# One load request per tensor for the first batch of an RWKV-5 plus mixer kernel

## The chip, the cores and the metric

The kernel runs on one core of a Trainium2 chip. The metric is device time in microseconds (us) of one execution; three runs of the kernel before the change are given. A core has five engines that each work through their own instructions in order: PE (TensorE, matmuls), DVE (VectorE), ACT (ScalarE), POOL (GpSimd) and SP (SyncE, here only a queue of DMA requests). An engine stops at an instruction whose inputs have not come, and everything behind it on that engine stops with it.

## The reference

Inputs `r`, `k`, `v` have the shape (4 batches, 8 heads, 768 steps, 48), `w` and `u` the shape (8, 48), all float32. Batch by batch a linear attention with decay is computed, and its output goes through a token and channel mixer:

```python
for t in range(S):
    kt, vt, rt = (k[:, :, t], v[:, :, t], r[:, :, t])
    cur = np.einsum('bhd,bhe->bhde', u[None] * kt, vt)
    y[:, :, t] = np.einsum('bhd,bhde->bhe', rt, state + cur)
    state = w[None, :, :, None] * state + np.einsum('bhd,bhe->bhde', kt, vt)
...
h = np.maximum(xt @ w_tok1, 0.0) @ w_tok2
u = x + h.transpose(0, 2, 1)
h2 = np.maximum(u @ w_ch1, 0.0) @ w_ch2
return (u + h2).astype(np.float32)
```

`x` is `y` with the heads side by side, (4, 768, 384); `xt` is its transpose; the mixer's hidden sizes are 256 and 1536.

## The kernel before, in words

The 768 steps of a batch are cut into 6 chunks of 128 steps. For each chunk the kernel multiplies k and r with powers of the decay (into tiles `kr`, bf16), transposes both, makes scores k times r on PE (`at_ps`), masks them on DVE (`AT`), adds the product with v to the product of r with the running state (`y_ps`, `S`, `kv_ps`), and adds the step's own term: `pr` is a product of the transposed k and r, `ad_ps` sums it with u, `adg` is that sum copied, and `yd` or `ydb` is v scaled by it. v is cast to bf16 first (`vb`). The result of a chunk is `x_b`. After the six chunks of a batch comes its mixer: `h_ps<-x_b,wtok` and `hx_ps` (token mixing, weights `wtok1`, `wtok2`), then `z_ps` (up, weights `wch1` in two parts) with a relu into `zr`, then `h_ps<-wch,zr` (down, weights `wch2` in three parts). A `zr` tile has 128 partitions of 12 x 384 bf16, and there are three buffers of it.

Every piece of work is a task made by `add` (line 215) or `flex` (line 222, which takes the engine from the table `ENGINES`). The table `ORDER` (line 21) is the order in which all tasks are emitted, so it sets each engine's order, SP's queue among them. `BUFS` (line 66) names for each pool the buffer that each use takes; a load into a buffer waits until the earlier user of that buffer is done. `kt` and `vt` have six buffers each, `win` three.

For the first two batches (style 'f32') r is read in windows of 256 steps (tile `win`, function `window`, line 558; steps 2p and 2p+1 lie side by side in partition p, so a row in memory is 384 bytes), and k and v by chunks (tiles `kt`, `vt`, line 493; rows of 192 bytes). That makes 15 requests for the first batch: 3 of 384 KB and 12 of 192 KB. SP issues them in this order: r of window 1, r of window 0, k of chunks 1 and 0, r of window 2, k 4, v 3, k 3, k 2, v 1, v 0, k 5, v 2, v 4, v 5. The loads of the second batch follow at their own places in `ORDER`.

The products are `mul_r` (line 561) and `mul_k` (line 794), the cast is `copy_v` (line 798); `turn_k`, `evac_k` and `product` (lines 806, 811, 815) transpose k (`trk`), copy it out of PSUM (`rka`) and make `pr`.

The mixer's seven weight loads (`load_weights`, line 532) are issued by POOL in its own order, each behind a wait for the landing of the load that `W_DEP` (line 173) names as (batch, chunk, 0 for k, 1 for r, 2 for v): both `wtok` parts wait for k of chunk 2, both `wch1` parts for v of chunk 0, and the three `wch2` parts for v of chunk 1, k of chunk 0 and v of chunk 5 of the second batch.

In the profile nearly every instruction has line 278, the helper that all engines are called through, so groups are told apart by tile names.

Of the kernel before, what the change touches and what calls it, by code (L numbers as in the profile page):

```python
# [11 lines left out]
f32 = mybir.dt.float32  # L12
# [6 lines left out]
Ln = ACTF.Ln  # L19

ORDER = [
# [43 lines left out]
]  # L65
BUFS = {
    'AT0': [
# [23 lines left out]
],  # L91
    'krw': [],
    'kt': [
    0, 1, 2, 3, 4, 5, 0, 1, 2, 3, 4, 5, 0, 2, 1, 3, 4, 5, 0, 2, 1, 3, 4, 5,
],
    'ku': [
    0, 1, 2, 0, 1, 2, 0, 2, 1, 0, 1, 0,
# [46 lines left out]
],  # L144
    'vb2': [],
    'vt': [
    0, 1, 2, 3, 4, 5, 0, 1, 2, 3, 4, 5, 0, 1, 2, 3, 4, 5, 0, 1, 2, 3, 4, 5,
],
    'win': [
    0, 1, 2, 0, 1, 2,  # L150
],
    'yd': [
    0, 1, 2, 0, 1, 2, 0, 1, 2, 1, 0, 2, 0, 2, 1, 0, 1, 0,
# [2 lines left out]
    0, 1, 0, 0, 1, 0,  # L156
],
    'zr': [
    0, 1, 2, 1, 0, 2, 1, 2,
],  # L160
}
ENGINES = [
# [9 lines left out]
]  # L172
W_DEP = [(0, 2, 0), (0, 2, 0), (0, 0, 2), (0, 0, 2), (1, 1, 2), (1, 0, 0), (1, 5, 2)]
GATES = {(2, 1, 0): 0, (3, 2, 1): 6}
NWARM = 13
WIDE_AT = [
# [63 lines left out]
def kernel(  # L240
# [14 lines left out]
    B, H, S, D = r.shape  # L255
    dm = H * D
    T = 128
    C = S // T
# [42 lines left out]
    def mul(on, out, a, c):  # L301
        engine_of[on].tensor_mul(out, a, c)
# [8 lines left out]
    def h3(t):  # L311
        return t.rearrange("p (h d) -> p h d", h=H)
# [177 lines left out]
    def two_steps(b, c, i):  # L490
        return (b, c // 2) in PAIRED or (i == 1 and wide(b))

    def load(b, c, i):
        nm, src = (("kt", k), ("rt", r), ("vt", v))[i]
        win = two_steps(b, c, i)
        nm = "win" if win else nm

        def f():
            if win:
                t = sb("win", [128, H, 2 * D], f32)  # L500
                dst = t
                what = src[b, :, ds(c * T, 2 * T), :].rearrange("h (p j) d -> p h (j d)", j=2)
            else:
                t = sb(nm, [128, dm], f32)
                dst = h3(t)
                what = src[b, :, ts(c, T), :].rearrange("h s d -> s h d")
            asked[b, c, i] = sp.dma_start(dst, what)
            loaded[b, c, i] = t
            if (b, c, i) in GATES:
                after(asked[b, c, i], sent[GATES[b, c, i]])  # L510

        return add("SP", "load2" if win else "load", f, [], take=(nm,))

    for b in range(B):
        for c in range(C):
            for i in range(3):
                if c % 2 and two_steps(b, c, i):
                    t_load[b, c, i] = t_load[b, c - 1, i]
                else:
                    t_load[b, c, i] = load(b, c, i)  # L520
# [261 lines left out]
    def unit(b, c):  # L782
# [10 lines left out]

        def mul_k(on):
            L["kr"] = krs[plan.buf("kp")]
            mul(on, L["kr"][:, 0, :, 0:D], h3(loaded[b, c, 0]), h3(wn[G][:, g, :]))

        def copy_v(on):
            L["vb"] = sb("vb", [128, dm], bf16)
            copy(on, L["vb"], loaded[b, c, 2])  # L800

        t_kp = flex(PRODUCT, mul_k, [lk, t_wn[G][g]] + t_kp0, take=("kp",), use=[(lk, "kt")])
        t_vb = flex({"ACT": "copy384", "DVE": "cast384"}, copy_v, [lv], take=("vb",), use=[(lv, "vt")])
# [34 lines left out]
        else:  # L838
            def mul_u(on):
                L["ku"] = sb("ku", [128, dm], f32)  # L840
                mul(on, L["ku"], loaded[b, c, 0], u_bc)

            def mul_rku(on):
                L["rku"] = sb("rku", [128, dm], f32)
                mul(on, L["rku"], L["ku"], loaded[b, c, 1])

            def sum_rku():
                L["adg"] = sb("adg", [128, H], f32)
# [4 lines left out]
            t_ad = add("DVE", "sum384", sum_rku, [t_rku], take=("adg",), use=[(t_rku, "rku")])  # L853

            def mul_r(on):
                mul(on, L["kr"][:, 1, :, 0:D], h3(loaded[b, c, 1]), h3(wp[:, g, :]))

            t_rp = flex(PRODUCT, mul_r, [lr, t_wp[g], t_kp], use=[(lr, "rt"), (t_kp, "kp")])
            if STYLE[n][0] == "dma":
# [344 lines left out]
```

## Time and profile before

| | |
|---|---|
| runs, us | 165.03, 164.47, 167.47 (median 165.03) |
| span of the profiled execution, us | 167.1 |
| granted TensorE clock, mean | 0.959 |
| moved by DMA | 26.89 MB, mean 161 GB/s |
| k loads: issue to landing, median | 5.0 us |
| v loads: issue to landing, median | 4.6 us |
| windows of r: issue to landing, median | 4.2 us |

The profiled execution is one of its own: the trace gives its span from the first to the last instruction and no time around it. Its span lies 2.1 us above the median of the three runs and 0.4 us below the highest of them.

How to read the views: a timeline row has start (us), duration (us), engine, line, operation, out tile<-in tile, shape, count, and in brackets the idle time of the engine just before it with what ended it. A row that merges several instructions has their common span. A row of a table by stretches has the stretch, its length, for each engine the busy time in it with the number of instructions, then the granted clock (1.00 is full), the busy share of the DMA engines and the rate in GB/s.

### The profile page before, as it was taken

Reading aid. Unit: us, or ns where it says so; the run is one execution under the profiler, and the core shown is the slowest. Engines: PE = TensorE matmul, PEld = TensorE weight load, DVE = VectorE, ACT = ScalarE, POOL = GpSimd, SP = SyncE. Lnnn points to the kernel's source line nnn. Section 1 sums busy time; section 2 is a strip of 40 time slices with the busy share of each in tenths; the row PEclk is TensorE's granted clock in tenths of the full one; section 3 lists DMA queues with packets and bytes.
Section 4 is the critical chain, followed back from the end, with each engine's and each line's share of the span. In section 5 each row is a group of like instructions: output and inputs, shape, how many; then the busy total and the mean of one; then the engine's idle time right before and its main releaser. Section 6 shows DMA issues by size and latency. Waiting matters only on the chain.

```text
span 167.1 us, 3776 instructions
## 1 busy us (share of the span) xinstructions
PE 156.7 (94%) x1459; PEld 105.0 (63%) x1459; DVE 122.7 (73%) x241; ACT 68.6 (41%) x157; POOL 80.5 (48%) x102
## 2 busy tenths in 40 slices
PE   6969999999999799799959999999999999999992
PEld 1347767677767577576625766577667566776662
DVE  6579996667999396799997898997989555411322
ACT  3957763565831332443601214077813101682100
POOL 7268969003598294999928895753211000000000
PEclk9985589999999999999987999999999999999999
DMA  5999999999899789999969996699990237100222
GB/s 131 224 201 187 189 237 234 214 181 215 172 190 181 151 183 160 214 198 186 209 131 215 188 177 140 100 229 232 243 187 25 94 94 184 52 2 4 94 94 94
DMA packets 93061, 26.89 MB, mean 161 GB/s; under 512 B 87794, under 2 KB 92148, under 8 KB 93044
## 3 DMA queue, kind: packets, MB, share of 16 engines
q1 hardware_dynamic: 90688, 23.40, 72.7%
q0 software_dynamic: 2160, 3.15, 10.8%
q8 instruction: 11, 0.18, 0.4%
q10 hardware_dynamic: 196, 0.11, 0.2%
q14 instruction: 6, 0.05, 0.1%
HBM read 20.46 MB, written 4.72 MB: 151 GB/s over the span
## 4 chain that ended last, share of the span: by engine, by line
PE 66%; DMA 10%; DVE 9%; POOL 5%; SPq 3%; issue 2%; ACT 2%; ACTq 0%
PE h_ps L278 26%; PE z_ps L278 23%; DMA kt<-in_k_dram 6%; PE y_ps L278 4%; DMA wch<-in_moe_w_ch_dram 4%; DVE kr L278 3%; PE hT_ps L278 3%; SPq L278 3%; PE at_ps L278 3%; PE kv_ps L278 2%; PE hx_ps L278 2%; DVE zr L278 2%; DVE AT L278 2%; POOL kr L278 2%; PE trk L278 2%
## 5 line engine op out<-in xcount | busy, mean ns | idle before, releaser
L278 PE MATMUL h_ps<-wch,zr 128*128 128x384 bf16 (+1 forms) x300 | 54.8, 326 | 1.0 <-DMA wch<-in_moe_w_ch_dram 0.9
L278 PE MATMUL z_ps<-uT,wch 128*128 128x384 bf16 x288 | 51.6, 326 | 2.1 <-DVE zr L278 2.1
L278 ACT ACTIVATE zr<-z_ps 128x384 bf16<-128x384 f32 x61 | 29.2, 491 | 35.4 <-PE z_ps L278 35.2
L278 PEld LDWEIGHTS <-wch 128*128 128x128 bf16 x288 | 31.5, 114 | 14.8 <-issue 2.6
L278 PEld LDWEIGHTS <-zr 128*128 128x128 bf16 x300 | 28.0, 99 | 17.9 <-issue 2.9
L278 DVE TENSOR_TENSOR AT<-at_ps,mask 128x512 bf16<-128x512 f32 x48 | 31.0, 682 | 0.9 <-PE at_ps L278 0.9
L278 DVE TENSOR_SCALAR zr<-z_ps 128x384 bf16<-128x384 f32 x35 | 18.6, 552 | 9.3 <-PE z_ps L278 7.8
L278 POOL TENSOR_TENSOR yd<-vb,adg 128x384 f32<-128x384 bf16 x16 | 13.4, 839 | 18.8 <-DVE adg L278 8.2
L278 POOL TENSOR_TENSOR kr<-kt,wnat 128x384 bf16<-128x384 f32 x15 | 15.7, 1052 | 10.2 <-DMA kt<-in_k_dram 10.1
L278 DVE TENSOR_TENSOR osb<-u_sb,h_ps 128x384 f32<-128x384 bf16 (+1 forms) x16 | 8.3, 526 | 11.8 <-PE h_ps L278 11.5
L278 PEld LDWEIGHTS <-kr 128*128 128x128 bf16 x176 | 12.9, 107 | 6.5 <-DVE kr L278 2.1
L278 POOL TENSOR_TENSOR ku<-kt,u_bc 128x384 f32<-128x384 f32 x11 | 12.1, 1105 | 4.7 <-DMA kt<-in_k_dram 4.7
L278 DVE TENSOR_TENSOR x_b<-y_ps,yd 128x384 bf16<-128x384 f32 x18 | 9.5, 550 | 2.9 <-PE y_ps L278 2.8
L278 POOL TENSOR_TENSOR kr<-rt,wp 128x384 bf16<-128x384 f32 x10 | 10.4, 1047 | 2.5 <-DMA rt<-in_r_dram 2.5
L278 DVE TENSOR_TENSOR kr<-kt,wnat 128x384 bf16<-128x384 f32 x9 | 9.7, 1078 | 2.6 <-DMA kt<-in_k_dram 2.6
L278 ACT CAST vb<-vt 128x384 bf16<-128x384 f32 x21 | 10.6, 516 | 2.6 <-DMA vt<-in_v_dram 2.5
L278 PEld LDWEIGHTS <-wtok 128*128 128x128 bf16 x78 | 7.5, 98 | 4.6
L278 ACT CAST S<-kv_ps 48x192 bf16<-48x192 f32 x20 | 6.2, 312 | 9.1 <-PE kv_ps L278 5.0
L278 PE MATMUL y_ps<-vb,AT 128*128 128x48 bf16 x192 | 9.0, 186 | 0.0
L278 DVE TENSOR_TENSOR u_sb<-x_b,hT_ps 128x384 bf16<-128x384 bf16 x15 | 7.6, 548 | 1.6 <-PE hT_ps L278 1.4
L278 PE MATMUL h_ps<-x_b,wtok 128*128 128x384 bf16 x48 | 8.8, 326 | 0.0
L278 POOL TENSOR_TENSOR kr<-win,wpair 128x384 bf16<-128x384 f32 x6 | 5.9, 996 | 4.5 <-DMA win<-in_r_dram 3.6
(95 smaller groups left out, 195.1 us busy)
## 6 DMA issues: line engine op xcount, KB each, us to landing
kt<-in_k_dram SPq DMA_DIRECT2D x24, 192.0 KB, 5.0
vt<-in_v_dram SPq DMA_DIRECT2D x24, 192.0 KB, 4.6
out_dram<-osb SPq DMA_DIRECT2D x23, 192.0 KB, 2.1
win<-in_r_dram SPq DMA_DIRECT2D x6, 384.0 KB, 4.2
rt<-in_r_dram SPq DMA_DIRECT2D x12, 192.0 KB, 4.3
wch<-in_moe_w_ch_dram POOLq DMA_DIRECT2D x4, 384.0 KB, 7.1
wtok<-in_moe_w_tok_dram POOLq DMA_DIRECT2D x2, 384.0 KB, 6.8
wch<-in_moe_w_ch_dram POOLq DMA_DIRECT2D x1, 768.0 KB, 9.4
```

The source lines that it names most:

```text
L278: return lambda *args, **kw: tc.keep_in_program_order(f(*args, **kw))
```

## The change

For batch 0 the 15 loads become three, one for each of r, k and v, each of a whole tensor (1152 KB, the same rows of 384 and 192 bytes). They take a buffer of `zr` each: r takes buffer 1, k buffer 0, v buffer 2, at SP's first three places, in the order r, k, v. The products, the cast and `window` read slices of these tiles, so k and v of a chunk are eight runs of 48 numbers in a partition where they were 384 in a row. The first four weight loads wait for v of batch 0. All other tasks keep their order (the tables only lose the 12 tasks and are numbered anew), and `kt`, `vt` and `win` keep their numbers of buffers.

```diff
     'kt': [
-    0, 1, 2, 3, 4, 5, 0, 1, 2, 3, 4, 5, 0, 2, 1, 3, 4, 5, 0, 2, 1, 3, 4, 5,
+    0, 1, 2, 3, 4, 5, 0, 2, 1, 3, 4, 5, 0, 2, 1, 3, 4, 5,
...
     'win': [
-    0, 1, 2, 0, 1, 2,
+    0, 1, 2,
...
     'zr': [
-    0, 1, 2, 1, 0, 2, 1, 2,
+    1, 0, 2, 0, 1, 2, 1, 0, 2, 1, 2,
...
-W_DEP = [(0, 2, 0), (0, 2, 0), (0, 0, 2), (0, 0, 2), (1, 1, 2), (1, 0, 0), (1, 5, 2)]
+W_DEP = [(0, 0, 2), (0, 0, 2), (0, 0, 2), (0, 0, 2), (1, 1, 2), (1, 0, 0), (1, 5, 2)]
...
+    def whole(b, i):
+        def f():
+            src = (k, r, v)[i][b]
+            if i == 1:
+                t = sb("zr", [128, H, C // 2, 2 * D], f32)
+                what = src.rearrange("h (w p j) d -> p h w (j d)", p=128, j=2)
+            else:
+                t = sb("zr", [128, H, C, D], f32)
+                what = src.rearrange("h (c p) d -> p h c d", p=128)
+            asked[b, i] = sp.dma_start(t, what)
+            for c in range(C):
+                asked[b, c, i] = asked[b, i]
+                loaded[b, c, i] = t[:, :, c // 2, :] if i == 1 else t[:, :, c, :]
+
+        return add("SP", "load_all", f, [], take=("zr",))
...
-                if c % 2 and two_steps(b, c, i):
+                if b == 0:
+                    t_load[b, c, i] = t_load[b, 0, i] if c else whole(b, i)
+                elif c % 2 and two_steps(b, c, i):
...
-            mul(on, L["kr"][:, 0, :, 0:D], h3(loaded[b, c, 0]), h3(wn[G][:, g, :]))
+            mul(on, L["kr"][:, 0, :, 0:D], loaded[b, c, 0], h3(wn[G][:, g, :]))
...
-            copy(on, L["vb"], loaded[b, c, 2])
+            copy(on, h3(L["vb"]), loaded[b, c, 2])
```

More of the change, by code (lines that the diff above doesn't have):

```diff
@@ L146 @@
     'vt': [
-    0, 1, 2, 3, 4, 5, 0, 1, 2, 3, 4, 5, 0, 1, 2, 3, 4, 5, 0, 1, 2, 3, 4, 5,
+    0, 1, 2, 3, 4, 5, 0, 1, 2, 3, 4, 5, 0, 1, 2, 3, 4, 5,
 ],
     'win': [
-    0, 1, 2, 0, 1, 2,
+    0, 1, 2,
 ],
@@ L507, in f @@
             asked[b, c, i] = sp.dma_start(dst, what)
-            loaded[b, c, i] = t
+            loaded[b, c, i] = t if win else h3(t)
             if (b, c, i) in GATES:
@@ L840, in mul_u @@
                 L["ku"] = sb("ku", [128, dm], f32)
-                mul(on, L["ku"], loaded[b, c, 0], u_bc)
+                mul(on, h3(L["ku"]), loaded[b, c, 0], h3(u_bc))
             def mul_rku(on):
                 L["rku"] = sb("rku", [128, dm], f32)
-                mul(on, L["rku"], L["ku"], loaded[b, c, 1])
+                mul(on, h3(L["rku"]), h3(L["ku"]), loaded[b, c, 1])
             def sum_rku():
@@ L855, in mul_r @@
             def mul_r(on):
-                mul(on, L["kr"][:, 1, :, 0:D], h3(loaded[b, c, 1]), h3(wp[:, g, :]))
+                mul(on, L["kr"][:, 1, :, 0:D], loaded[b, c, 1], h3(wp[:, g, :]))
             t_rp = flex(PRODUCT, mul_r, [lr, t_wp[g], t_kp], use=[(lr, "rt"), (t_kp, "kp")])
```

85 rows, old and new, of the table ORDER are left out of this document.

## The prediction

> **What bounds the kernel now.** I read the page's head first, then its chain, then the engines by stretches, and last the timelines of the front, where the change is.
>
> ```profile
> span 167.1 us, 3776 instructions
> ...
> PE 156.7 (94%) x1459; PEld 105.0 (63%) x1459; DVE 122.7 (73%) x241; ACT 68.6 (41%) x157; POOL 80.5 (48%) x102
> ...
> PE 66%; DMA 10%; DVE 9%; POOL 5%; SPq 3%; issue 2%; ACT 2%; ACTq 0%
> ```
>
> PE is busy for 94% of the span and two thirds of the chain are PE. Where the remaining 6% lie is told by the stretches (columns: stretch, length, busy time and count of PE, PEld, DVE, ACT, POOL, granted clock, DMA share, GB/s).
>
> ```profile
> 2.00:5.00 3.00, 3.00 (x6) 0.93 (x6) 2.69 (x18) 1.98 (x3) 2.11 (x12) 1.00 1.05 251
> 3.00:4.00 1.00, 1.00 (x3) 0.13 (x2) 1.00 (x9) 0.09 (x1) 0.93 (x9) 1.00 1.17 325
> 4.00:5.00 1.00, 1.00 (x3) 0.30 (x2) 0.86 (x7) 0.97 (x2) 0.29 (x1) 1.00 1.28 268
> 10.00:17.00 7.00, 5.55 (x54) 3.69 (x53) 5.85 (x12) 4.33 (x15) 6.40 (x8) 0.61 1.45 186
> 17.00:22.00 5.00, 4.81 (x66) 3.78 (x63) 4.75 (x9) 3.81 (x10) 4.54 (x7) 0.52 1.44 192
> 22.00:36.00 14.00, 13.57 (x166) 9.79 (x166) 10.20 (x20) 6.76 (x16) 6.38 (x8) 1.00 1.16 228
> 26.00:54.00 28.00, 27.92 (x294) 20.01 (x292) 21.92 (x42) 13.91 (x33) 14.83 (x18) 1.00 1.03 196
> 54.00:58.00 4.00, 3.07 (x34) 2.04 (x33) 1.65 (x4) 1.56 (x3) 1.39 (x2) 1.00 0.89 175
> 58.00:66.00 8.00, 8.00 (x106) 5.76 (x104) 6.65 (x15) 2.91 (x8) 5.51 (x6) 1.00 0.97 172
> 66.00:70.00 4.00, 3.14 (x31) 2.09 (x30) 2.68 (x4) 1.12 (x3) 3.52 (x3) 1.00 0.88 166
> ...
> 82.00:90.00 8.00, 5.79 (x38) 3.07 (x37) 8.00 (x12) 1.41 (x3) 4.12 (x5) 0.79 0.78 171
> 90.00:164.00 74.00, 74.00 (x633) 49.82 (x631) 48.73 (x91) 24.77 (x57) 20.88 (x22) 1.00 0.61 127
> ```
>
> Two things are to be seen. From 26 us PE hardly rests: 0.9 us idle in 54 to 58, 0.9 in 66 to 70, 2.2 in 82 to 90, and none in the 74 us from 90 to 164. So a delay ahead of 26 us can be won back only in those 4.0 us and in the half clock of 82 to 90; else it reaches the end. And from 2 to 22 us, while batch 0 is read, the DMA engines have a busy share above 1 all the time: rows of 384 bytes came at 325 and 268 GB/s, rows of 192 bytes at 186 to 192.
>
> Now the requests of the front, and who waits for them.
>
> ```profile
> 0.81 1.07 SPq L278 DMA_DIRECT2D win<-in_r_dram  x2
> ...
> 6.68 1.09 SPq L278 DMA_DIRECT2D vt<-in_v_dram  x1
> ...
> 13.49 3.07 SPq L278 DMA_DIRECT2D vt<-in_v_dram  x3
> 16.68 0.92 SPq L278 DMA_DIRECT2D kt<-in_k_dram  x1
> ```
>
> ```profile
> 11.83 0.51 ACT L278 CAST vb<-vt 128x384 bf16<-128x384 f32 x1 [1.77 <-DMA vt<-in_v_dram]
> 12.24 0.34 ACT L278 ACTIVATE lnwd<-wd_ps 64x4 f32<-64x4 f32 x2
> 12.61 0.48 ACT L278 COPY u_bc<-u_ps 128x384 f32<-128x384 f32 x1
> 12.99 0.30 ACT L278 ACTIVATE wG<-lnwd 128x4 f32<-128x4 f32 x2
> 13.19 0.60 ACT L278 ACTIVATE wp<-lnw,iota 128x384 f32<-128x384 f32 x1
> 14.19 0.61 ACT L278 ACTIVATE wp<-lnw,iota 128x384 f32<-128x384 f32 x1 [0.40 <-PE ud_ps L278]
> 15.27 0.58 ACT L278 COPY rka<-trk 128x512 bf16<-128x512 bf16 x1 [0.47 <-PE trk L278]
> ```
>
> ```profile
> 7.24 0.56 DVE L278 TENSOR_TENSOR kr<-kt,wnat 128x384 bf16<-128x384 f32 x1 [0.52 <-DMA kt<-in_k_dram]
> ...
> 10.76 1.35 DVE L278 TENSOR_TENSOR kr<-kt,wnat 128x384 bf16<-128x384 f32 x1 [1.22 <-DMA kt<-in_k_dram]
> ...
> 16.12 0.41 DVE L278 TENSOR_TENSOR pr<-trk,rkb 128x512 bf16<-128x512 bf16 x1
> ```
>
> The requests were ordered so that each chunk comes shortly before its use: the first product of k runs at 7.24, the first cast of v (chunk 3) at 11.83. That cast stands in ACT's queue ahead of `u_bc`, `wG`, `wp`, the copy `rka` of chunk 3 and everything later, so what v waits for, ACT waits for.
>
> **The change part by part.** *Landing times.* The bytes are the same, 1.18 MB each for r, k and v, and so are the rows in memory; SP's 15 requests become three, and the DMA engines were already full with the small ones. r alone: about 0.75 MB by 5.0 (251 GB/s from 2.0), the other 0.42 MB at 268 GB/s, so it lands at 6.6. k at the 186 of 10 to 17: 1.18/0.186 = 6.3 us, lands at 12.9. v the same again: 19.3. As a check on the sum, the whole of batch 0 is read by about 19 us before too; its last v was issued in 13.49 to 16.56. The end is not later; what is lost is that chunk 3 of v came at 11.83 and now nothing of v comes before 19.3.
>
> *k.* DVE stands at its first product of k from 7.24 to 12.9. Its work from there to the product `pr` of chunk 3 took 16.12 - 7.24 = 8.9 us, of which 1.2 was waiting for k: it could be at `pr` at 12.9 + 7.7 = 20.6.
>
> *v.* ACT stands at the first cast till 19.3. From there to the start of `rka` is 15.27 - 11.83 = 3.44 us, less the two waits 0.40 and 0.47 that fall away since PE is long done: 2.6. With 0.58 for `rka` itself, DVE gets it at 19.3 + 2.6 + 0.6 = 22.5, after the 20.6 of the path through k. So v decides, and `pr` moves from 16.12 to 22.5: 6.3 us later (6.33 unrounded). Of k's delay nothing adds to it.
>
> *Does it stay 6.3?* From 16 to 22 DVE is nearly full (4.75 of 5.00 in 17 to 22), and it takes up its queue behind `pr` at the same pace. POOL comes along: its `wGm` waits for ACT's `wG`.
>
> ```profile
> 13.98 1.61 POOL L278 TENSOR_TENSOR wGm<-bm,wG 128x384 f32<-128x384 f32 x2
> ...
> 17.27 1.02 POOL L278 DMA_DIRECT2D wtok<-in_moe_w_tok_dram  x1
> ...
> 21.08 0.82 POOL L278 TENSOR_TENSOR ydb<-vb,adg 128x384 bf16<-128x384 bf16 x1 [0.44 <-PE y_ps L278]
> 21.86 0.81 POOL L278 DMA_DIRECT2D wch<-in_moe_w_ch_dram  x1
> ```
>
> PE's first uses of the weights, the landings of the first `wtok` and the first `wch` (last column), and PE's only wait for a weight:
>
> ```profile
> 25.53 1.14 PE L278 MATMUL h_ps<-x_b,wtok 128*128 128x384 bf16 x6
> ...
> 31.62 3.09 PE L278 MATMUL z_ps<-uT,wch 128*128 128x384 bf16 x18
> ```
>
> ```profile
> wtok<-in_moe_w_tok_dram POOLq DMA_DIRECT2D x1, 384.0 KB, 6.7
> ```
>
> ```profile
> wch<-in_moe_w_ch_dram POOLq DMA_DIRECT2D x1, 384.0 KB, 8.0
> ```
>
> ```profile
> PE h_ps L278 <- DMA wch<-in_moe_w_ch_dram: 0.9, 1, 0.9
> ```
>
> `wG`, 1.2 behind the cast, now ends at 19.3 + 1.2 + 0.3 = 20.8, so POOL is 6.8 late there and loses the excess over 6.3 in its own idle time (the 0.44 ahead of 21.08).
>
> *The weights' new wait.* Behind it on POOL stand the products of k and the `ydb` of batch 0. It costs nothing: POOL reaches the first `wtok` at 17.27 + 6.8 = 24.1, when v has been there for 4.8 us. That cover would be gone if v landed after 24. `wtok` lands at 24.1 + 6.7 = 30.8, and its first use is at 25.53 + 6.3 = 31.8; the first `wch` at 21.86 + 6.4 + 8.0 = 36.3 for a use at 31.62 + 6.3 = 37.9. Covers of 1.0 and 1.6 us: thin, the first thing to be late next.
>
> *SP's queue.* The loads of batch 1 now stand right behind three requests instead of 15 and need no buffer that batch 0 holds, so the DMA engines stay full after 19.3, and about 1 MB of batch 1 is in before the weights start at 24.1 (4.8 us at 192 GB/s), where before none was. Batch 1's loads thus come early against the work; what that can give back is PE's wait for `wch` (0.9) and part of the other idle times. Since each of these follows from PE, POOL and DVE work that itself moves by 6.3, I take nothing; the bounds are 0 and 4.0.
>
> *Strided slices.* A product of k now reads runs of 48; the windows of r were read so before, and cost the same:
>
> ```profile
> L278 DVE TENSOR_TENSOR kr<-win,wpair x6: 548/550/557, 6.2 to 39.1; 128x384 bf16<-128x384 f32 x6
> ```
>
> ```profile
> L278 DVE TENSOR_TENSOR kr<-kt,wnat x9: 541/557/3890, 7.2 to 114.1; 128x384 bf16<-128x384 f32 x9
> ```
>
> Nothing, then. For ACT's cast no such row is at hand; between its 0.51 and the 0.61 of `wp`, six casts cost 0 to 0.6 us; I take 0, since their sizes are as small as the products'. A gain from fewer issues on SP is nothing either: SP is not what the front waits for.
>
> *Sum.* Front +6.3, later stages 0, weights 0, slices 0: the profiled execution would go from a span of 167.1 to 173.4. No time around that span is shown; it lies 2.1 above the median of the runs, 165.03, and the front's term does not depend on that: 165.0 + 6.3 = 171.3 us.
>
> **The rivals.** *Faster: large requests run faster.* If the whole-tensor requests kept the best rate of the front, 325 GB/s, r would land at 5.6, k at 9.3, v at 12.9; then `pr` would be at 16.1 through ACT and at 17.0 through k, a loss of 0.9, and with batch 1 far ahead the 4.0 us of PE idle and some 1.7 of half clock in 82 to 90 ((1 - 0.79) x 8) could vanish: 165.0 + 0.9 - 5.7 = 160.2. It decides from about 270 GB/s up, where the loss is 2.3 and, with all of the later 5.7 gone, 161.6 is left. Against it: the 192-byte rows of twelve requests ran at 186 GB/s with the engines' share at 1.45 and no gap between requests, so there is nothing between them to save. The Trainium skill, DMA: Bandwidth & Descriptors, section Bandwidth, asks for requests of 1 MiB and more and gives 2.0 us plus bytes over 436 GB/s for one; as an estimate from that page, v would be in at 0.8 + 2.0 + 3 x 2.7 = 10.9, and the change would cost nothing. The trace differs: the rate of 186 holds for many requests in flight, so the row decides.
>
> *The delay is won back.* The front is 6.3 late, but loads that come early remove PE's idle times after 54 us (4.0) or the half clock in 82 to 90: 165.0 + 6.3 - 4.0 = 167.3, which is within 2%. For it: PE's wait of 0.9 for `wch`. Against it: the largest of these, in 82 to 90, is behind DVE, busy for all 8.00, and not behind a load.
>
> *More is lost.* If the long requests run at 172 GB/s, the rate of 58 to 66, v lands at 20.3, a microsecond more; if the clock returns to full only inside the mixer, more again. PE had the half clock from 12 to 22 (0.61 and 0.52) and full from 22; that rise moves to about 28, and a half clock in PE-bound work as long as that in 82 to 90 costs the same 1.7; weights that are late past their cover add one. 171.3 + 1.0 + 1.7 + 1.0 = 175.0. The Trainium skill, TensorE: Matmul & The Clock Gate, section What's actually happening, lets the clock rise after about 3.4 us of sustained work; here PE was busy from 12 to 22 and the clock rose only at the end, so the trace does not agree for sparse work.
>
> **How the numbers follow.** My forecast (165 plus 4 to 8) has 0.70, more lost 0.16, won back 0.10, faster 0.04. The time is 171.3. The range runs from 167.3 (won back) to 175.0 (all that can be late): 167.3 to 175.0; its lower end also covers k and v at the 251 GB/s of 2 to 5 (v at 16.1, `pr` at 19.2, a loss of 3.1: 168.1). A measurement of this kernel tells about 2%, 3.3 us, from no change: slower means above 168.3. Slower 0.86 (forecast and more lost), same 0.10, faster 0.04.
>
> **What would show it.** Right: r landing near 6.6, k near 12.9, v near 19.3; DVE idle some 5 us ahead of its first product of k; ACT idle for 3 us or more ahead of the first `vb` with DMA of v as releaser; `pr` of chunk 3 at 22 to 23; the first `h_ps` at 31 to 33 and the first `z_ps` near 38; PE full from there. Wrong: v landing by 14; a first `z_ps` near 32; or PE idle after 40 us shrinking by more than 3 us. New waits of PE for `wtok` or `wch` would mean that the thin covers broke.

## The result and the profile after

| | before | after |
|---|---|---|
| median of the runs, us | 164.75 (164.30 to 167.47, 4 runs) | 173.06 (170.39 to 175.09, 4 runs) |
| after over before | | 1.0414, 95% interval 1.0308 to 1.0519 |
| profiled execution: time, span, us | no time shown, 167.1 | 174.03, 172.3 |
| first `vb`, ACT starts at | 11.83 | 20.96 |
| `pr` of chunk 3, DVE starts at | 16.12 | 24.18 |
| first `z_ps`, PE starts at | 31.62 | 39.37 |

The change makes the kernel slower by 4.1%. Two of the four runs of after, the profiled one among them, lie more than 1.5% above its fastest run and are not counted in the ratio, and such runs are not counted further down either; that is why the ratio (0.0414 x 164.75 = 6.8 us, interval 5.1 to 8.6) is less than the difference of the medians (8.3).

The head of the page after, to lay beside that of before:

```profile
span 172.3 us, 3754 instructions
...
PE 155.3 (90%) x1459; PEld 104.9 (61%) x1459; DVE 121.3 (70%) x241; ACT 68.5 (40%) x157; POOL 80.1 (46%) x102
```

No engine got more work; PE's share fell from 94% to 90%. The stretches say where PE waits (stretch, length, busy time and count of PE, PEld, DVE, ACT, POOL, granted clock, DMA share, GB/s):

```profile
2.00:5.00 3.00, 3.00 (x6) 0.93 (x6) 2.69 (x18) 1.98 (x3) 2.11 (x12) 1.00 0.82 225
5.00:8.00 3.00, 2.82 (x7) 0.76 (x5) 0.00 (x0) 3.00 (x7) 0.00 (x0) 1.00 1.13 247
8.00:10.00 2.00, 0.00 (x0) 0.00 (x0) 0.56 (x1) 1.16 (x3) 1.48 (x2) 1.00 1.05 191
10.00:13.00 3.00, 0.00 (x0) 0.00 (x0) 0.00 (x0) 0.00 (x0) 2.19 (x3) 1.00 1.11 183
13.00:17.00 4.00, 1.50 (x15) 1.53 (x16) 2.20 (x5) 0.02 (x1) 0.35 (x1) 1.00 1.09 189
17.00:19.00 2.00, 2.00 (x15) 1.80 (x13) 2.00 (x4) 0.99 (x1) 0.65 (x1) 1.00 1.12 188
...
82.00:90.00 8.00, 7.85 (x80) 5.44 (x79) 7.74 (x12) 3.72 (x9) 8.00 (x9) 1.00 1.05 209
```

Between 8 and 13 us PE does nothing, DVE one product, and ACT has 1.16 us of work, while the DMA share stays above 1. The bytes come at the rate that the prediction took: summed over the stretches, 3.48 MB are there at 19.0 and the 3.54 MB of r, k and v at 19.3. The signals come later. Time from issue to landing of the three requests (their KB column counts only one row's bytes), and two engines that wait for them:

```profile
zr<-in_r_dram SPq DMA_DIRECT2D x1, 0.4 KB, 7.5
...
zr<-in_k_dram SPq DMA_DIRECT2D x1, 0.2 KB, 12.5
...
zr<-in_v_dram SPq DMA_DIRECT2D x1, 0.2 KB, 15.4
```

```profile
0.87 0.88 SPq L277 DMA_DIRECT2D zr<-in_r_dram  x1
2.21 2.86 SPq L277 DMA_DIRECT2D zr<-in_k_dram  x1
5.52 6.55 SPq L277 DMA_DIRECT2D zr<-in_v_dram  x1
12.12 6.23 SPq L277 DMA_DIRECT2D kt<-in_k_dram  x1
```

```profile
14.80 0.56 DVE L277 TENSOR_TENSOR kr<-zr,wnat 128x384 bf16<-128x384 f32 x1 [5.77 <-DMA zr<-in_k_dram]
...
24.18 0.41 DVE L277 TENSOR_TENSOR pr<-trk,rkb 128x512 bf16<-128x512 bf16 x1
```

```profile
20.96 0.51 ACT L277 CAST vb<-zr 128x384 bf16<-128x384 f32 x1 [2.98 <-DMA zr<-in_v_dram]
...
23.44 0.58 ACT L277 COPY rka<-trk 128x512 bf16<-128x512 bf16 x1
```

So r landed at 0.87 + 7.5 = 8.4, k at 2.21 + 12.5 = 14.7, v at 5.52 + 15.4 = 20.9. DVE idles 5.77 us ahead of its first product of k, ACT 2.98 ahead of the first cast, both released by DMA. Further on, PE's rows:

```profile
39.37 3.09 PE L277 MATMUL z_ps<-uT,wch 128*128 128x384 bf16 x18
...
63.76 0.81 PE L277 MATMUL h_ps<-wch,zr 128*128 128x384 bf16 x4 [0.43 <-DMA wch<-in_moe_w_ch_dram]
...
78.67 3.58 PE L277 MATMUL z_ps<-uT,wch 128*128 128x384 bf16 x21
...
91.98 0.65 PE L277 MATMUL z_ps<-uT,wch 128*128 128x384 bf16 x3 [2.13 <-DVE zr L277]
93.38 2.76 PE L277 MATMUL h_ps<-wch,zr 128*128 128x384 bf16 x16
```

The same instructions of before:

```profile
56.52 0.81 PE L278 MATMUL h_ps<-wch,zr 128*128 128x384 bf16 x4 [0.93 <-DMA wch<-in_moe_w_ch_dram]
...
69.74 0.99 PE L278 MATMUL hx_ps<-wtok,h1r 128*128 128x384 bf16 x5 [0.86 <-DVE h1r L278]
...
72.19 3.58 PE L278 MATMUL z_ps<-uT,wch 128*128 128x384 bf16 x21
...
85.50 0.65 PE L278 MATMUL z_ps<-uT,wch 128*128 128x384 bf16 x3 [2.12 <-DVE zr L278]
86.89 4.33 PE L278 MATMUL h_ps<-wch,zr 128*128 128x384 bf16 x16
```

Read as a difference, after is 7.75 us late at the first `z_ps` (39.37 - 31.62), 7.24 at 63.76, 6.48 at 78.67 and at 91.98. Half a microsecond came back at the wait for `wch` (0.43 where it was 0.93); by 78.67 another 0.8, and before's wait of 0.86 for `h1r` has no counterpart. The wait of 2.1 behind DVE stayed. The last step, 16 `h_ps` in 2.76 us where before took 4.33, is the half clock of before's traced execution in 82 to 90 (granted 0.79, after 1.00); with it the difference shrinks to 4.9 (the spans differ by 5.2), and it is no effect of the change that could be relied on.

These gains belong to the one traced execution of before and not to the change. Two of the experiments below wait for the weights in the same way and use the same buffers, and differ only in the requests of the first batch: e1 has those of before, e3 those of after. Their PE rows, first e1 (span 161.7), then e3 (span 170.8):

```profile
31.28 3.09 PE L278 MATMUL z_ps<-uT,wch 128*128 128x384 bf16 x18
...
82.55 2.77 PE L278 MATMUL h_ps<-wch,zr 128*128 128x384 bf16 x16
```

```profile
39.53 3.09 PE L277 MATMUL z_ps<-uT,wch 128*128 128x384 bf16 x18
...
90.89 2.77 PE L277 MATMUL h_ps<-wch,zr 128*128 128x384 bf16 x16
```

Here e3 is 8.25 us late at the first `z_ps`, 8.34 at the 16 `h_ps` and 9.1 at the end: nothing is won back. e1 has no wait for `wch`, 0.19 for `h1r` where before had 0.86, and no wait of 2.1 behind DVE. That last wait follows one long DVE product, first in after, then in e1:

```profile
87.56 3.90 DVE L277 TENSOR_TENSOR kr<-kt,wnat 128x384 bf16<-128x384 f32 x1
```

```profile
79.28 1.01 DVE L278 TENSOR_TENSOR kr<-kt,wnat 128x384 bf16<-128x384 f32 x1
```

POOL works on products of its own beside both. The long form stands in the traces of before (3.89, the largest of its row in the prediction), after and e6 (3.92), with a wait of PE of 2.1 each time, and in no other; why it comes in some executions only is open. With one trace for each kernel, differences of about 2 us between two spans can be this alone.

### The profile page after: what moved, and what is told of

Same layout as the page of the kernel before. It is cut to its first block, busy times and chain, and to the rows that moved or that the text cites. A ratio compares the mean times of both kernels' runs of the same rounds, so it can differ in the third digit from the quotient of the medians.

```text
span 172.3 us, 3754 instructions
## 1 busy us (share of the span) xinstructions
PE 155.3 (90%) x1459; PEld 104.9 (61%) x1459; DVE 121.3 (70%) x241; ACT 68.5 (40%) x157; POOL 80.1 (46%) x102
## 3 DMA queue, kind: packets, MB, share of 16 engines
q0 software_dynamic: 2160, 3.15, 10.7%
## 4 chain that ended last, share of the span: by engine, by line
PE 66%; DMA 11%; DVE 10%; POOL 5%; issue 4%; ACT 2%; SPq 1%; POOLq 0%; DVEq 0%
PE h_ps L277 25%; PE z_ps L277 22%; DMA zr<-in_k_dram 7%; PE y_ps L277 4%; DMA wch<-in_moe_w_ch_dram 3%; PE hT_ps L277 3%; DVE AT L277 3%; DVE kr L277 3%; PE at_ps L277 3%; PE kv_ps L277 2%; PE hx_ps L277 2%; POOL yd L277 2%; DVE zr L277 2%; PE trk L277 2%; PE tr_ps L277 2%
## 5 line engine op out<-in xcount | busy, mean ns | idle before, releaser
L277 PE MATMUL h_ps<-wch,zr 128*128 128x384 bf16 (+1 forms) x300 | 53.2, 320 | 0.5 <-DMA wch<-in_moe_w_ch_dram 0.4
L277 PEld LDWEIGHTS <-zr 128*128 128x128 bf16 x300 | 27.5, 98 | 16.3 <-issue 0.7
L277 POOL TENSOR_TENSOR kr<-kt,wnat 128x384 bf16<-128x384 f32 x12 | 12.5, 1047 | 0.8 <-DMA kt<-in_k_dram 0.8
L277 PE MATMUL trk<-ident,kr 128*128 128x128 bf16 x48 | 5.6, 250 | 7.8 <-DVE kr L277 7.7
L277 ACT COPY rkb<-tr_ps 128x1024 bf16<-128x1024 bf16 x4 | 4.0, 1012 | 11.4 <-PE tr_ps L277 11.0
L277 ACT CAST vb<-vt 128x384 bf16<-128x384 f32 x15 | 7.4, 513 | 1.1 <-DMA vt<-in_v_dram 1.1
```

Of the source, the lines that this page charges most:

```text
L277: return lambda *args, **kw: tc.keep_in_program_order(f(*args, **kw))
```

## The experiments

In the tables and in the text a *wall* is the earliest moment at which one input's path lets `pr` of chunk 3 and the first `z_ps` begin.

Theory: a whole-tensor request gives nothing until its last byte, so the first-used chunk waits for the last; v, third in line, decides through ACT's queue. Rivals: k alone is the cause; r is; the plain order r, k, v is (small requests would do as badly); the weights' new wait; the slices and buffers.

In most experiments `whole` was replaced by a list of requests, issued at the place of the first load, into the same slices of the same three `zr` tiles. "Small" requests are the old ones: two chunks of r, one of k or v. In the edits R, K and V stand for the code's 1, 0 and 2, and `ALL`, `R_SMALL`, `K_SMALL` and `V_SMALL` for lists that the code writes out.

| kernel | r, k, v | median of the counted runs, us | ratio to before, 95% interval | `pr` of chunk 3 | first `z_ps` |
|---|---|---|---|---|---|
| before | small, old order | 164.47 | | 16.12 | 31.62 |
| e1_old_order | small, old order | 164.92 | 1.0021 (0.9983 to 1.0060) | 15.37 | 31.28 |
| e2_rkv_small | small, small, small | 166.51 | 1.0166 (1.0085 to 1.0246) | 18.79 | 34.42 |
| e7_r_whole | whole, small, small | 168.88 | 1.0151 (1.0053 to 1.0249) | 21.12 | 37.51 |
| e10_k_whole | small, whole, small | 171.26 | 1.0316 (1.0205 to 1.0427) | 21.77 | 37.23 |
| e6_v_small | whole, whole, small | 174.12 | 1.0485 (1.0297 to 1.0673) | 22.55 | 37.99 |
| e9_v_whole | small, small, whole | 171.74 | none | 23.69 | 39.99 |
| e5_k_small | whole, small, whole | 172.88 | 1.0408 (1.0326 to 1.0490) | 24.61 | 40.54 |
| after | whole, whole, whole | 171.25 | 1.0414 (1.0308 to 1.0519) | 24.18 | 39.37 |

The last two columns are of one traced execution each. Each ratio is to runs of before taken beside that kernel's own. For e9 no ratio was formed; its four runs lie between 171.56 and 176.02.

**The old requests in the old order, but into `zr`** (e1_old_order; the weights wait as in before)

```diff
+FIRST = [(R, (2, 3)), (R, (0, 1)), (K, (1,)), (K, (0,)), (R, (4, 5)), (K, (4,)), (V, (3,)),
+         (K, (3,)), (K, (2,)), (V, (1,)), (V, (0,)), (K, (5,)), (V, (2,)), (V, (4,)), (V, (5,))]
-W_DEP = [(0, 0, 2), (0, 0, 2), (0, 0, 2), (0, 0, 2), ...
+W_DEP = [(0, 2, 0), (0, 2, 0), (0, 0, 2), (0, 0, 2), ...
```

> Buffers of zr, strided slices and unhindered loads of batch 1 as in the changed kernel, but the first batch is read by the 15 requests of before in their order, and the weights wait as before. Theory (v is late as a whole and ACT stands at its first cast): the front is as before, first z_ps at 31 to 32, time 164 to 165.5. Rival (slices or buffers cost): first z_ps near 39, time above 170. Rival (early loads of batch 1 help later): first z_ps as before, and 1 to 2 us less at the end, 163 to 164.

Measured 1.0021 (0.9983 to 1.0060). Buffers and strided slices are worth nothing that can be seen. Batch 1's loads are issued here as in before (its first at 16.81 and 16.68), so this run says nothing on their early start.

**Small requests in the order r, k, v** (e2_rkv_small)

```diff
+FIRST = [(R, (2, 3)), (R, (0, 1)), (R, (4, 5)),
+         (K, (1,)), (K, (0,)), (K, (4,)), (K, (3,)), (K, (2,)), (K, (5,)),
+         (V, (3,)), (V, (1,)), (V, (0,)), (V, (2,)), (V, (4,)), (V, (5,))]
```

> The 15 small requests, but in the order of the changed kernel: all of r, then all of k, then all of v, chunk 3 of v first. Theory: chunk 3 of v lands near 15 where the whole v landed at 20.9; first cast 3 us later than before, pr of chunk 3 about 2.3 us later, time 166.5 to 168. If the order alone made the loss: as the changed kernel, 172 to 173. If the size of the requests alone made it: as before, 165.

1.0166, and the first `z_ps` 2.8 us later than before. The cast of v waits here too, but till 15.33 instead of 20.96, since its chunk is the first of v to come:

```profile
15.33 0.51 ACT L278 CAST vb<-zr 128x384 bf16<-128x384 f32 x1 [2.88 <-DMA zr<-in_v_dram]
```

Of the 7.75 us the order alone is 2.8; the size of the requests is the rest.

**The first two weights behind k again** (e3_old_wdep)

```diff
-W_DEP = [(0, 0, 2), (0, 0, 2), (0, 0, 2), (0, 0, 2), ...
+W_DEP = [(0, 2, 0), (0, 2, 0), (0, 0, 2), (0, 0, 2), ...
```

> The changed kernel with the first two weights behind k, as before (the other two behind v, as before). Theory: POOL reaches the first wtok after v has landed anyway, so first z_ps at 39 to 39.5 and 172 to 173, no change. Rival (the new wait of the weights holds POOL): first wtok issued near 17 to 20 and 166 to 168.

Ratio 1.0469 (1.0389 to 1.0549), first `z_ps` at 39.53: no gain. The first `wtok` was issued at 25.51 instead of 25.80: POOL's own queue sets that time, not the wait.

**The first cast of v behind the copy of chunk 3** (e4_cast_later; one task moved in `ORDER`)

```diff
-    ... 190, 187, 121, 26, 48, 171, 117, 27, ...
+    ... 190, 187, 121, 26, 48, 117, 27, ...
...
-    ... 52, 128, 139, 123, 173, 894, ...
+    ... 52, 128, 139, 123, 173, 171, 894, ...
```

> The changed kernel, with one task moved: ACT's first cast of v (chunk 3) stands behind its copy rka of chunk 3 and no longer ahead of lnwd, u_bc, wG, wp and rka. Theory (it is ACT's order behind v that is late): ACT does these from 18 on, pr of chunk 3 comes at 22 to 23 and not at 24.2, bounded by the path through k; first z_ps 1 to 2 us earlier than 39.4; time 1 to 2 us below the changed kernel. Rival (v is needed by PE just as late anyway, or k is what binds): first z_ps at 39 to 39.5, no change.

`pr` moved by 0.3 us (24.06 in e3, whose first product of k starts at the same 14.4, to 23.75), the first `z_ps` stands at 39.71, no earlier than in after, and the ratio is 1.0419 (1.0348 to 1.0491): a miss. With ACT out of the way the chain of k on PE came out nearly as late. Its first product starts at 14.45, and `u_ps` took 1.62 us where e6, at the faster clock, took 0.89:

```profile
18.25 1.62 PE L280 MATMUL u_ps<-wp,ones 1*128 1x384 f32 x2
```

```profile
18.60 0.89 PE L278 MATMUL u_ps<-wp,ones 1*128 1x384 f32 x2
```

The path through k is therefore 7.6 us long (e6) or 9.3 (23.75 - 14.45), as PE's clock stands. That v's delay travels through ACT's queue is read from the rows of after; since k's wall stood right behind it, this run neither shows nor refutes it.

**The same with 16 more warm matmuls ahead of the first transposes** (e8_warm)

```diff
-NWARM = 13
+NWARM = 29
...
-    ... 134, 893, 28, 151, 136, 118, ...
+    ... 134, 893, 28, 151, 896, 897, 898, 899, 900, 901, 902, 903, 904, 905, 906, 907, 908, 909, 910, 911, 136, 118, ...
```

> The changed kernel with the first cast of v behind rka, as in the earlier run, and 16 more warming matmuls of 512 columns ahead of PE's first transposes, which fill PE's wait for k. Theory B says that PE's chain from the landing of k, about 9 us at half clock, is the wall: with the clock kept full, pr of chunk 3 comes at 21.5 to 23 where it came at 23.75, first z_ps at 37 to 38.5, time 169 to 170.5. Rival (not PE's clock but DVE's and ACT's own work after k): first z_ps at 39.3 to 39.8, 171.4.

No gain that can be told: ratio 1.0376 (1.0209 to 1.0543), `pr` at 23.84, first `z_ps` at 39.43. The warm matmuls were over by 12.0, PE then idled 3.59 us for k, and after one fast group the transposes ran at half pace again. Inconclusive on the clock, since the warmth did not reach the work.

**One tensor small or whole at a time** (e5_k_small, e6_v_small, e7_r_whole, e9_v_whole, e10_k_whole)

```diff
+ALL = (0, 1, 2, 3, 4, 5)
+R_SMALL = [(R, (2, 3)), (R, (0, 1)), (R, (4, 5))]
+K_SMALL = [(K, (c,)) for c in (1, 0, 4, 3, 2, 5)]
+V_SMALL = [(V, (c,)) for c in (3, 1, 0, 2, 4, 5)]
+FIRST = [(R, ALL)] + K_SMALL + [(V, ALL)]      # e5_k_small
+FIRST = [(R, ALL), (K, ALL)] + V_SMALL         # e6_v_small
+FIRST = [(R, ALL)] + K_SMALL + V_SMALL         # e7_r_whole
+FIRST = R_SMALL + K_SMALL + [(V, ALL)]         # e9_v_whole
+FIRST = R_SMALL + [(K, ALL)] + V_SMALL         # e10_k_whole
```

> The changed kernel with k in six requests of a chunk each (chunks 1, 0, 4, 3, 2, 5), r and v whole, same order r, k, v. Theory A (v alone decides): v still lands near 20.7, first z_ps at 39 to 39.5, time 171 to 173. Theory B (two walls of equal height: whole k delays PE's transposes at half clock, whole v delays ACT, each enough alone): also 39 to 39.5. Rival C (k alone decides, v costs next to nothing): first z_ps at 34.5 to 36, time 166 to 168.

> The changed kernel with v in six requests (chunks 3, 1, 0, 2, 4, 5), r and k whole. Theory A (v alone decides): chunk 3 of v lands near 15.5, the front is bound by the path through k as the prediction reckoned it, first z_ps at 36 to 37.5, time 168 to 169.5. Theory B (two walls): k's chain on PE at half clock stays, first z_ps at 38.3 to 39.5, time 170.5 to 172.5. Rival C (k alone): as B.

> Only r is whole; k and v are in six requests each behind it (k 1, 0, 4, 3, 2, 5, then v 3, 1, 0, 2, 4, 5). Beside the run with all three in small requests in this order (first z_ps 34.4, 166.5 us) it shows what a whole r costs by itself. Theory: r lands at 7 to 8.4 and k's first chunk at 9 to 9.5 anyway, so first z_ps at 34.4 to 35.2, time 166.5 to 167.5. Rival (the first products of r bind): 36 or more.

> Only v is whole; r comes in three requests and k in six ahead of it (r, k 1, 0, 4, 3, 2, 5, then v). Staircase theory (whole r, whole k and whole v each set a wall, and the highest one counts; the wall of v is 39.4 to 40.5): v lands near 20.7, first z_ps at 39.3 to 40.5, time 171 to 173, though r and k are as early as in the run with 15 small requests. Rival (the losses of the three add up, v's share being the 1.4 by which the run with v alone in small requests was faster): first z_ps near 36, time 168.

> Only k is whole, behind r in three requests and ahead of v in six (3, 1, 0, 2, 4, 5). Staircase theory: k lands near 14.5, the wall of k stays as in the run with r and k whole, first z_ps at 37.5 to 38.3, time 169.5 to 172. Rival (there it was the whole r that bound): first z_ps at 34.5 to 36, time 166.5 to 168.

The delays are walls, of which the highest counts: they do not add. Over e2's 34.42, whole r alone (e7) costs 3.1 us at the first `z_ps`, whole k alone (e10) 2.8 and whole v alone (e9) 5.6, and all three together (after) 5.0. Whole v alone (e9) puts `z_ps` at 39.99, as late as all three (39.37), and small k beside whole v (e5, 40.54) helps nothing: "k alone" is refuted. Without whole v (e6) it is 37.99, between the two bands expected there; whole k alone (e10) gives 37.23. The wall of v as e9 shows it, ACT's cast and DVE's product of chunk 3:

```profile
20.30 0.51 ACT L278 CAST vb<-zr 128x384 bf16<-128x384 f32 x1 [7.77 <-DMA zr<-in_v_dram]
```

```profile
23.69 0.41 DVE L278 TENSOR_TENSOR pr<-trk,rkb 128x512 bf16<-128x512 bf16 x1
```

The wall of k as e10 shows it, DVE's first product of k and `pr` of chunk 3:

```profile
14.22 0.56 DVE L278 TENSOR_TENSOR kr<-zr,wnat 128x384 bf16<-128x384 f32 x1 [7.41 <-DMA zr<-in_k_dram]
...
21.77 0.42 DVE L278 TENSOR_TENSOR pr<-trk,rkb 128x512 bf16<-128x512 bf16 x1
```

The counted runs scatter by up to 2.6 us within a kernel (e6: 172.83 and 175.40) and put e6 above e9; the order of the walls rests on the traces, and the ratios of e5, e6, e10 and after are not told apart. PE's clock differs between the traces too: `u_ps` took 0.89 in e6 and e10, and 1.62 in e2, e5, e7 and e9. At the slower clock the path through k is 1.7 us longer (9.3 against 7.6), so the walls of k and of v lie closer together than 37.23 and 39.99, as e4 found.

e7 was a miss: whole r alone reached 37.51. Its DVE and POOL rows show why:

```profile
10.28 1.35 DVE L278 TENSOR_TENSOR kr<-zr,wpair 128x384 bf16<-128x384 f32 x1
11.55 1.34 DVE L278 TENSOR_TENSOR kr<-zr,wnat 128x384 bf16<-128x384 f32 x1
12.82 1.76 DVE L278 TENSOR_TENSOR kr<-zr,wpair 128x384 bf16<-128x384 f32 x1
```

```profile
8.58 3.90 POOL L278 TENSOR_TENSOR kr<-zr,wpair 128x384 bf16<-128x384 f32 x3 [4.28 <-DMA zr<-in_r_dram]
```

r lands in one piece at 8.5, so POOL's three products of r start together and run beside DVE's, which take 1.34 to 1.76 us instead of 0.55. To test that, the next run leaves POOL's products of r for the first batch out and writes zeros in their place, so its result lacks these parts:

**e7 with POOL's products of r left out** (e11_pool_zero)

```diff
-    mul(on, W["kr"][:, j, :, 0:D], loaded[b, 2 * w, 1][:, :, j * D:(j + 1) * D], h3(wp2[:, j, :]))
+    if b == 0 and on == "POOL":
+        pool.memset(W["kr"][:, j, :, 0:D], 0.0)
+    else:
+        mul(on, W["kr"][:, j, :, 0:D], loaded[b, 2 * w, 1][:, :, j * D:(j + 1) * D], h3(wp2[:, j, :]))
```

> The run with only r whole, without POOL's three products of r for the first batch: POOL writes zeros into these halves of kr, so the outputs of that batch lack parts of r. It tells why a whole r cost 3.1 us in the first z_ps. Theory (POOL's products, released late and all at once by the whole r, run beside DVE's products of r and k and stretch these from 0.55 to 1.35 us): DVE's products take 0.55 again, the third product of k ends 2 to 2.7 us earlier than 15.4, first z_ps at 35 to 36, time 166.5 to 168. Rival (r's own landing is what costs): DVE's products end where they did, first z_ps at 37 to 37.6.

```profile
10.32 0.55 DVE L278 TENSOR_TENSOR kr<-zr,wpair 128x384 bf16<-128x384 f32 x1
10.79 0.55 DVE L278 TENSOR_TENSOR kr<-zr,wnat 128x384 bf16<-128x384 f32 x1
11.26 0.55 DVE L278 TENSOR_TENSOR kr<-zr,wpair 128x384 bf16<-128x384 f32 x1
```

The products are back at 0.55 and `z_ps` at 34.75, near e2's 34.42. So what whole r costs the front, 3 us at the first `z_ps`, comes in the main from DVE and POOL in each other's way and not from waiting for r: the third of these products ends at 14.58 in e7 and at 11.81 here, 2.8 earlier, and PE waits for DVE there. A part may be PE's clock, since `u_ps` took 1.62 in e7 and 0.90 here. In the times of the runs nothing of it is seen: the ratio is 1.0159 (1.0114 to 1.0203), beside e7's 1.0151. The Trainium skill, SBUF — State Buffer, section Who interferes with whom, says that a DVE instruction with two SBUF inputs contends with a GpSimd instruction that reads SBUF, and not with one that only writes. The trace agrees: 0.55 against 1.34 and more beside POOL's products. Since POOL's memsets here ran at 4.25, they show nothing on writes.

**Nothing queued behind v** (e12_hold: batch 1's first load waits for v)

```diff
             asked[b, c, i] = sp.dma_start(dst, what)
             loaded[b, c, i] = t if win else h3(t)
+            if "held" not in asked:
+                asked["held"] = asked[b, c, i]
+                after(asked[b, c, i], asked[0, 2])
```

> The changed kernel with one wait more: SP's first load of batch 1 waits until v of batch 0 has landed, so that nothing follows v in the DMA queues. In the changed kernel that load was issued from 12.12 us on, and v landed at 20.9 where the bytes, added up by stretches, had reached 3.54 MB at 19.3. Theory A, the 1.6 us are time in which the sixteen engines already work on the next requests while some still carry v (engines not in step): without followers the same engines still carry the same rows, but the rate falls off between 18 and 21 us, the last bytes of v move up to about 20.5 to 20.9, and the landing stays at 20.5 to 21. Theory B, followers take part of the rate from v: without them v lands at 19.3 to 19.7, pr of chunk 3 starts at 22.5 to 22.9. Theory C, a fixed time between the last byte and the signal: the bytes reach 3.54 MB at 19.3, nothing moves from there to 20.9, and v lands at 20.9. The time: 172 to 174 by A and C, 171 to 173 by B; batch 1's loads come 3 us or more later than in the changed kernel, which by the experiment with the old order was worth nothing.

The DMA rate as v ends, and the cast:

```profile
19.20:19.40 0.20, 0.20 (x1) 0.00 (x1) 0.20 (x1) 0.00 (x0) 0.00 (x0) 1.00 0.98 161
19.40:19.60 0.20, 0.20 (x5) 0.20 (x5) 0.20 (x1) 0.00 (x0) 0.00 (x0) 1.00 0.72 115
19.60:19.80 0.20, 0.20 (x7) 0.20 (x5) 0.03 (x1) 0.00 (x0) 0.00 (x0) 1.00 0.51 85
19.80:20.00 0.20, 0.20 (x7) 0.20 (x5) 0.16 (x1) 0.00 (x0) 0.00 (x0) 1.00 0.22 38
20.00:20.40 0.40, 0.25 (x5) 0.07 (x2) 0.40 (x2) 0.00 (x0) 0.00 (x0) 1.00 0.02 4
```

```profile
20.70 0.51 ACT L277 CAST vb<-zr 128x384 bf16<-128x384 f32 x1 [2.62 <-DMA zr<-in_v_dram]
```

The rate falls off over 0.6 us (the busy share of the DMA engines goes from 0.98 to 0.22, so they do not finish together), the last bytes move at about 20.0, and the cast starts 0.7 later. Theories A and C hold a part each; B, that the followers take v's rate, would have had v at 19.3 to 19.7 and is refuted as the main cause. The Trainium skill, DMA: Bandwidth & Descriptors, says in the section Why a DMA increments its semaphore by 16 and not by 1 that the engines of one request finish independently and the semaphore counts them. The trace agrees: the rate tapers over 0.6 us, and the reader starts only after the last of it. The lag behind the mean rate is 1.1 us here (by 19.0 the stretches sum to 3.44 MB; the last 0.10 at 187 GB/s would be in at 19.6), 1.6 in after; the other half microsecond is not settled. The kernel took 171.62 us, 1.0451 (1.0339 to 1.0564), beside 1.0414 for after, with batch 1's first load issued at 20.70 and not at 12.12: the early start of these loads brings no gain that the times show. (The expectation above took that from e1, which cannot show it.) Of PE's waits one is longer than in after, 0.8 where that had 0.43:

```profile
PE h_ps L277 <- DMA wch<-in_moe_w_ch_dram: 0.8, 1, 0.8
```

## Why the prediction was right, and where its size was off

Forecast 171.3 (range 167.3 to 175.0), measured 173.06 as the median of all four runs and 171.25 as that of the two counted; slower, as 0.86 of the chance had it. That 171.3 came so close is in part luck: the term of 6.3 for the front measured 7.8 to 8.3 at the first `z_ps`, and the loss of the counted runs is only known to lie between 5.1 and 8.6.

- **The bound.** PE full from 26 us, so a delay of the front reaches the end. Right: the 8.25 us between e1 and e3 at the first `z_ps` are 9.1 at the end of the traces, and 7.4 between the medians of their counted runs (164.92 and 172.31). e7 fits less well, 5.9 at the first `z_ps` (37.51 - 31.62) and 2.5 by its ratio (0.9 to 4.1); why is open.
- **Landing times: the step that failed.** "r lands at 6.6, k at 12.9, v at 19.3" were 8.4, 14.7 and 20.9. The bytes were right (3.54 MB at 19.3); the step took the moment at which the mean rate has delivered a request's bytes for the moment at which its reader may start. e12 shows the difference for v. The profile of before had it: the request that its first cast of v, at 11.83, waits for comes after three windows of r and three chunks of k, with itself 1.97 MB; by the prediction's own rates these are in at 6.6 for r and then 0.79/0.186 = 4.2 us more, at 10.8, and the cast ran 1.0 later.
- **The path through v.** ACT 2.6 and `rka` 0.6, 3.15 unrounded: measured 24.18 - 20.96 = 3.22. Right. With v's 1.6 the front's term of 6.3 becomes 7.9; measured 8.06 at `pr`, 7.75 at the first `z_ps`.
- **The path through k.** 7.7 us: 7.55 in e10 (21.77 - 14.22) and 7.6 in e6 (22.55 - 14.95). "So v decides" held, but by less than the 1.9 us forecast when PE's clock was low: e4 found k's chain 0.3 us behind.
- **The weights' wait at nothing.** Right (e3). POOL reached the first `wtok` at 25.80, 1.7 later than forecast, and v had landed 4.9 before. No wait of PE for `wtok` arose.
- **Strided slices and cast at nothing.** Right: 0.55 to 0.56 and 0.51 (e1 as a whole 1.0021).
- **Later stages at nothing, between 0 and 4.0.** Right at nothing; the bound of 4.0 was wrong. It was the idle time of PE in before's one traced execution, and e1, with the same requests, has 0.3 of it (16.00 - 15.66 in 54 to 70, none in 82 to 90). The 1.3 us that after regained on before come from there, and e3 regained nothing on e1. Early loads of batch 1, the cause that was assumed, bring nothing that the runs show: PE's wait for `wch` is 0.9 in before, none in e1, 0.4 in after and e3, 0.8 in e12.
- **The rival "large requests run faster".** Refuted: 183 to 191 GB/s from 8 to 19 us, where before had 186 to 192. The estimate from the Trainium skill that stood there (DMA: Bandwidth & Descriptors; v in at 10.9) does not agree with the 20.9 measured; its formula stands in the section Anatomy of one DMA, for requests issued through GpSimd, while these are SP's, and only the rule of 1 MiB stands in the section Bandwidth.
- **"More is lost"** had one microsecond for v through a lower rate. The size was about right (1.6 measured), its cause was another: the rate held, the landing lagged. The rise of PE's clock did move as that rival had it, to about 29 us (granted 0.72 in 28 to 30, 1.00 from 30 on).

## What to carry to other kernels

A large request releases its readers only when all of it is there: reckon the landing of each request from all bytes ahead of it and add a microsecond or more for the tail, and when the queue is full anyway, issue the requests in the order and grain of their first use. Delays at the start were walls here, not a sum: find which input's path ends last, and expect the next wall close behind when that one is taken down. A landing in one piece also bunches the work behind it: DVE and POOL then work at the same time and slow each other, as e7 and e11 show. And lay more than one trace of the same requests side by side before a wait in one of them is taken as time to be won.

## What the runs showed of the hardware that was not expected

A whole request moves its rows in far fewer packets, at the same rate. The stretch 9 to 13 us of after, then 10 to 16 of before:

```profile
DMA packets 971, 0.74 MB, mean 185 GB/s; under 512 B 6, under 2 KB 971, under 8 KB 971
```

```profile
DMA packets 5914, 1.12 MB, mean 186 GB/s; under 512 B 5914, under 2 KB 5914, under 8 KB 5914
```

That is 760 bytes a packet instead of 190, about four rows of 192 bytes, at 185 and 186 GB/s. Fewer packets bought nothing, so their number does not set the rate; what does, the runs do not show.

PE can run at about half pace where the clock record says 1.00: e7's stretch from 8 to 36 us has granted 1.00, yet its `u_ps` took 1.62 us, the time of e4, against 0.89 in e6. In a front of short transposes the duration of one known matmul is the surer sign of the clock.
